# A gated scan with grouped experts: the units' instructions through the routing of the eleventh put down in front of the third early job's work

## The chip, the cores and the metric

The kernel runs on one core of one Trainium2 chip. The metric is device time in microseconds (us) from the start of the program to its end; several executions are taken and the median counts. A core has five engines with a queue of instructions each: TensorE (PE in the profile, its weight loads PEld), VectorE (DVE), ScalarE (ACT), GpSimd (POOL) and SyncE (SP), which here issues most of the DMA transfers. The engines wait for each other by semaphores.

## The reference

Two layers, one behind the other. The first is a gated scan over each of four sequences of 3648 tokens with 256 features; the second sends each of the 14592 resulting rows through one of 16 small networks.

```python
f = lower_bound + (1 - lower_bound) * sigmoid(f_logit)
for t in range(S):                                  # S = 3648, per sequence
    h = f[:, t] * h + (1 - f[:, t]) * x[:, t]
    y[:, t] = h
x = y.reshape(14592, 256)
g = argmax(x @ w_group)                             # 4 groups, weight g_w = its softmax
e = argmax(x @ w_expert[g])                         # 4 experts in a group, weight e_w
out[token] = g_w * e_w * (relu(x @ w1[g, e]) @ w2[g, e])   # 256 -> 1024 -> 256
```

## The kernel before

**Units.** The tokens are cut into 29 units of 512 (0 to 28). A unit is loaded (`p1_load`, 1 MB, tile zt; from unit 11 on by ScalarE's queue), gated on ScalarE (`p1_ta`, lines 189 and 199) and scanned on VectorE, once for each half of the features (`p1_tb`, lines 215 and 226). TensorE turns its rows (`p1_back`, two parts, line 253), computes its routing numbers (`p1_router`, line 267) and turns those (`p1_logits`, line 278). Units are routed in groups of mostly two: s1 to s6 on VectorE find each row's expert and its place in that expert's list, with one small pair of matmuls (s4, lines 313 and 314), and s7 scatters the rows, 128 at a time, into the lists xs in DRAM by indirect DMAs of GpSimd's queue (line 348). Units 9 and 10 are a group, 11 and 12 the next, and so on.

**Early jobs.** An expert's list is worked on before the scan is over. Each expert has one early job (A0 to A15) for its first rows: `EARLY` says after how many units the job's rows are taken (7, 7, 9, 9, 11, 11, 13, 15, 15, ...) and how many tiles of 128 rows they are (2, 2, 2, 2, 2, 2, 3, 3, 3, ...). At a cut u, `close_early(u)` fixes the places on VectorE and `early_rows(u)` loads the rows of all jobs of that cut (tile xr, line 805, on SP's queue); these loads wait for the scatters of all units below u. The cut 11 belongs to jobs A4 and A5, 13 to A6, 15 to A7 and A8. Behind the early jobs come the late ones, B0 to B15, for the rest of each list, once all units are routed.

**A job.** Its weights come in four pieces of 512 KB (tile st, line 823, on SP's queue, eight buffers: a piece is asked for when the piece eight places earlier has been split). Each piece is split into a high half on ScalarE (wh, line 831) and the rest on VectorE (wl, line 832). The job's rows are transposed by TensorE (line 885) and split as well (xh, line 894, on ScalarE; xl, line 895, on VectorE). The first layer goes in steps (`m1_step`; four for a job of 256 rows): twelve matmuls on lines 938 to 940, then relu on ScalarE (hh, line 943) and the low half on VectorE (hl, line 944). The second layer (`m2_step`, line 968, 24 matmuls for 128 rows) ends in a scaled copy on ScalarE (line 980) and a scatter of GpSimd's queue into the output (line 981). While a job is worked on, the next one is split and transposed.

**The order.** The units' work stands in one list of 424 items (`bgq`), in the order in which it must be put down; `marks[u]` is the number of the item `early_rows(u)`: 160 for the ninth, 212 for the eleventh, 239 for the thirteenth; `marks["order"]` is 424. In a loop over the jobs, `bg_step` puts down items between the jobs' steps so that each mark is reached by a due point, half a job before the job that needs it is prepared; `bg_to(n)` puts down all items up to n at once. `start_macro(mi + 1)` at the top of a job makes sure that the next job's rows have been asked for.

In the kernel before, the items stand like this around the third early job (A2; its steps are those of `mi == 2`): items up to 197 before A2's first step, 198 to 202 behind it, 203 to 206 behind the second, 207 to 210 behind the third, 211 to 214 behind the fourth. Item 193 and 195 are the scatters of units 9 and 10, 197 is `close_early(11)`, 212 is `early_rows(11)`.

SP's instructions keep the order in which the code puts them down for the whole kernel. TensorE's, VectorE's and ScalarE's keep it only before the loop over the jobs; in the loop the framework may let an instruction go ahead of one that was put down earlier, by when it expects their inputs. On the chip each engine then follows its own queue strictly.

Of the kernel before, what the change touches and what calls it, by code (L numbers as in the profile page):

```python
# [45 lines left out]
def gated_scan_moe(ctx: ExitStack, tc, zx, lower, wroute, wexp, out, S):  # L46
# [874 lines left out]
    def m1_step(j, ch, cs):  # L921
        if j.raw:
            return raw1(j, ch, cs)
        w = j.chunks[ch][1]
        if cs[0] == 0:
            j.hh[ch] = mo.tile([P, KF, 2 * P], F16, name="hh")
            j.hl[ch] = mo.tile([P, KF, 2 * P], BF16, name="hl")
            b, p, g = j.parts[ch][-1]
            if g > 1 and p < P // g:
                for t in (j.hh[ch], j.hl[ch]):  # L930
                    nc.vector.memset(t[:, :, w:w + P // g - p], 0.0)
        late[0] += j.kind == "B"
        pm = bank("m1" if late[0] % 2 == 0 else "p")
        xh, xl = j.xh[ch][:, :, 0:w], j.xl[ch][:, :, 0:w]
        for n, c in enumerate(cs):
            po = pm[:, n * w:(n + 1) * w]
            for k in range(KD):
                nc.tensor.matmul(po, w1_at(j.wh, k, c), xh[:, k], start=(k == 0), stop=False)  # L938
                nc.tensor.matmul(po, w1_at(j.wh, k, c), xl[:, k], start=False, stop=False)  # L939
                nc.tensor.matmul(po, w1_at(j.wl, k, c), xh[:, k], start=False, stop=(k == KD - 1))  # L940
        hi = j.hh[ch][:, cs[0]:cs[-1] + 1, 0:w]
        pv = pm[:, 0:len(cs) * w].rearrange("p (c w) -> p c w", w=w)
        nc.scalar.activation(hi, pv, AF.Relu)  # L943
        nc.vector.scalar_tensor_tensor(out=j.hl[ch][:, cs[0]:cs[-1] + 1, 0:w], in0=pv, scalar=0.0, in1=hi,  # L944
                                       op0=ALU.max, op1=ALU.subtract)
# [9 lines left out]
    def m2_step(j, ch, t, pm=None):  # L955
        b, p, g = j.parts[ch][t]
        begun = pm is not None
        pm = pm if begun else bank("m2")
        c0 = b - j.chunks[ch][0]
        q, dw = P // g, D // g  # L960
        n = p if g == 1 else q
        ts = slice(c0, c0 + n)
        if j.raw:
            raw2(j, ch, t, range(KF // 2 if begun else 0, KF), pm)
        for c in range(0 if j.raw else KF):
            for s, (h, w) in enumerate(((j.hh, j.wh), (j.hh, j.wl), (j.hl, j.wh))):
                for i in range(g):
                    nc.tensor.matmul(pm[i * q:i * q + n, 0:dw], h[ch][:, c, ts], w2_at(w, c)[:, i * dw:(i + 1) * dw],  # L968
                                     start=(c == 0 and s == 0), stop=(c == KF - 1 and s == 2),
                                     tile_position=(0, i * q) if g > 1 else None)  # L970
        o = mo.tile([P, D], F32, name="o", bufs=O_BUFS)
        if j.kind == "B":
            lt, r = j.info, b // P
            if g > 1:
                r += j.tails.index((b, p, g))
        else:
            pi = max(i for i, (a, _) in enumerate(j.pieces) if a <= b)
            lt, r = j.meta[pi], (b - j.pieces[pi][0]) // P
        s = slice(0, p if g == 1 else P)
        nc.scalar.activation(o[s, 0:dw], pm[s, 0:dw], AF.Copy, scale=lt.bitcast(F32)[s, r, 1:2])  # L980
        nc.gpsimd.indirect_dma_start(  # L981
            out=out_v[out_n[0]].rearrange("n (g d) -> (n g) d", g=g),
            out_offset=bass.IndirectOffsetOnAxis(ap=lt[s, r, 0:1], axis=0),
            in_=o[s, 0:dw], in_offset=None, bounds_check=g * N - 1, oob_is_err=False)
        out_n[0] += 1
# [19 lines left out]
    def first_parts():  # L1005
        out = []
        for (j,), u in zip(macros, PLAN):
            half = {}

            def begin(j=j, half=half):  # L1010
                half[0] = bank("m2")
                raw2(j, 0, 0, range(KF // 2), half[0])
            fs = [lambda j=j: job_xt(j, 0)]
            fs += [lambda j=j, cs=cs: m1_step(j, 0, cs) for cs in j.cols[0]]
            fs += [begin, lambda j=j, half=half: m2_step(j, 0, 0, half[0])]
            out += [(u, f) for f in fs]
        return out

    thunks, marks = p1_thunks(list(range(NU)), GROUPS, first_parts())
# [3 lines left out]
    def bg_pop():  # L1023
        done[0] += 1
        bgq.popleft()()

    def bg_to(n):
        while done[0] < n:
            bg_pop()
# [11 lines left out]
    def prep_thunks(j):  # L1041
        th = []

        def sp(i):
            if i == 2:
                live[0] += 1
            at = piece_index[(id(j), i)]
            fetch_to(max(at + 1, min(at + (4 if j.raw else STG_BUFS), pptr[0] + 2)))
            job_split(j, i)
            if i == 3 and j.kind == "B" and j.idx == 1:  # L1050
                leftovers()
            if i == 3 and j.kind == "B" and j.idx + 1 < NE:
                tail_blank(j.idx + 1)

        for i in range(4):
            f = lambda i=i: sp(i)
            f.held = i == 2
            th.append(f)
        for pi in range(len(j.pieces)):
            th.append(lambda pi=pi: job_xt(j, pi))  # L1060
        return th

    def start_macro(mi):
        mac = macros[mi]
        bg_to(marks[EARLY[mac[0].idx][0]] if mac[0].kind == "A" else marks["order"])
        for j in mac:
            if j.kind != "A" or j.idx == NE - 1:
                job_rows(j)

    def work(mac):  # L1070
        return sum(len(j.chunks) * KF + sum(len(p) for p in j.parts) for j in mac)
# [13 lines left out]
    def bg_step(q, left, n):  # L1085
        if q:
            for _ in range(-(-len(q) * n // max(1, left))):
                if q and not (getattr(q[0], "held", False) and live[0] >= 3):
                    q.popleft()()
        if bgq:  # L1090
            rate = max([(m - done[0]) / (a - now[0]) for a, m in due if a > now[0] and m > done[0]] or [0.0])
            credit[0] += rate * n
            while credit[0] >= 1 and bgq:
                credit[0] -= 1
                bg_pop()
        now[0] += n
# [13 lines left out]
    for mi, mac in enumerate(macros):  # L1110
        if mi < len(PLAN):
            continue
        q = deque()
        if mi + 1 < len(macros):
            start_macro(mi + 1)
            for j in macros[mi + 1]:
                q.extend(prep_thunks(j))
        left = work(mac)
        for j in mac:
            for ch in range(len(j.chunks)):  # L1120
                for cs in j.cols[ch]:
                    m1_step(j, ch, cs)
                    left -= len(cs)
                    bg_step(q, left - 2, len(cs))
                if pending is not None:
                    pj, pc = pending
                    for t in range(len(pj.parts[pc])):
                        m2_step(pj, pc, t)
                        left -= 1
                        bg_step(q, left - 2, 1)  # L1130
                    if pc == len(pj.chunks) - 1:
                        live[0] -= 1
                pending = (j, ch)
        while q:
            q.popleft()()
# [66 lines left out]
```

## Time and profile before

| | us |
|---|---|
| median of 3 runs (lowest to highest) | 775.78 (774.38 to 777.86) |
| the profiled execution's own time | 776.59 |
| its span (first to last instruction) | 774.8 |
| TensorE busy in it | 716.6 |
| VectorE busy in it | 533.9 |
| ScalarE busy in it | 458.8 |
| GpSimd busy in it | 286.6 |

The profile is one execution. A row of a timeline says when an instruction (or a run of equal ones) began, how long it took, its engine, line and tiles, and in brackets how long the engine had been idle before it and who ended that. A matmul's end is modelled. PEclk is the granted share of TensorE's clock: 1.00 is 2.4 GHz, 0.50 is 1.2 GHz.

### The profile page before, as it was taken

What the parts mean: (1) busy time and instruction counts of PE and PEld (TensorE: products, weight loads), DVE (VectorE), ACT (ScalarE), POOL (GpSimd) and SP (SyncE); (2) the same over time, 40 slices, a digit from 0 to 9 for tenths busy, and PEclk for the clock granted to TensorE, in tenths of its full rate; (3) what the DMA queues carried; (4) which work ended last, traced back from release to release, by engine and by line L of the source; (5) the groups of instructions that cost most, each with busy time, mean ns of one, the idle gap of its engine ahead of it and who ended that gap; (6) DMA issues with size and microseconds to landing.
All of it is one profiled execution on the core that took longest, in us unless ns stands there. A gap on an engine that the chain in (4) does not pass through costs nothing.

```text
span 774.8 us, 20906 instructions
## 1 busy us (share of the span) xinstructions
PE 716.6 (92%) x8055; PEld 633.7 (82%) x8055; DVE 533.9 (69%) x1046; ACT 458.8 (59%) x822; POOL 286.6 (37%) x272
## 2 busy tenths in 40 slices
PE   2656996989999999999999999999999999999995
PEld 1434885778888888889888898999999999999995
DVE  6898798898999976786465545555564676666640
ACT  6586785867878955455455444454555465555541
POOL 3663248276556543642111122213222322232222
PEclk9985998999999999999999999999999999999998
DMA  7998898889998845588656343553553556555300
GB/s 278 352 376 301 306 303 246 320 281 314 317 326 287 266 152 124 171 223 203 170 133 135 120 101 108 134 127 120 139 168 101 158 158 173 158 168 175 88 30 24
DMA packets 104037, 151.75 MB, mean 196 GB/s; under 512 B 63938, under 2 KB 73952, under 8 KB 100608
## 3 DMA queue, kind: packets, MB, share of 16 engines
q1 hardware_dynamic: 89248, 102.00, 45.3%
q0 software_dynamic: 11424, 30.02, 10.8%
q10 hardware_dynamic: 3264, 18.39, 6.9%
q8 instruction: 63, 1.03, 0.6%
q14 instruction: 38, 0.31, 0.1%
HBM read 112.69 MB, written 38.19 MB: 195 GB/s over the span
## 4 chain that ended last, share of the span: by engine, by line
PE 63%; DVE 11%; issue 10%; DMA 10%; POOL 4%; ACT 1%; SPq 0%; POOLq 0%; DVEq 0%; ACTq 0%
PE ps_m L968 29%; PE ps_m L938 7%; PE ps_m L939 7%; PE ps_m L940 7%; DMA xs<-rows,posi 4%; DMA zt<-in_zx_dram 3%; PE ps_p L938 3%; PE ps_p L940 3%; PE ps_p L939 3%; POOL out_dram L981 3%; DVE h L226 2%; DVE wl L832 2%; DMA xr<-xs 2%; PE ps_p L253 1%; DVE hl L944 1%
## 5 line engine op out<-in xcount | busy, mean ns | idle before, releaser
L968 PE MATMUL ps_m<-wh,hl 128*128 128x256 f16 (+4 forms) x1304 | 261.4, 251 | 0.0
L968 PE MATMUL ps_m<-wl,hh 128*128 128x256 bf16 (+4 forms) x1304 | 261.2, 250 | 0.1
L968 PE MATMUL ps_m<-wh,hh 128*128 128x256 f16 (+4 forms) x1304 | 261.1, 251 | 0.0
L968 PEld LDWEIGHTS <-hh 128*128 128x128 f16 (+2 forms) x2608 | 192.3, 99 | 23.4 <-issue 3.7
L938 PE MATMUL ps_m<-xh,wh 128*128 128x256 f16 (+11 forms) x766 | 192.7, 261 | 7.2 <-DVE hl L944 7.2
L939 PE MATMUL ps_m<-xl,wh 128*128 128x256 bf16 (+11 forms) x766 | 192.7, 261 | 0.3 <-DVE xl L895 0.3
L940 PE MATMUL ps_m<-xh,wl 128*128 128x256 f16 (+11 forms) x766 | 192.7, 261 | 0.0
L832 DVE TENSOR_TENSOR wl<-st,wh 128x1024 bf16<-128x1024 f32 x124 | 149.6, 1218 | 55.2 <-ACT wh L831 54.0
L348 POOL DMA_INDIRECT xs<-rows,posi x114 | 135.2, 1186 | 129.3 <-DVE rows L330 47.6
L981 POOL DMA_INDIRECT out_dram<-o,info x75 | 86.2, 1150 | 242.4 <-ACT o L980 221.1
L944 DVE SCALAR_TENSOR_TENSOR hl<-ps_m,hh 128x512 bf16<-128x512 f32 (+9 forms) x172 | 114.5, 668 | 74.5 <-ACT hh L943 73.7
L943 ACT ACTIVATE hh<-ps_m 128x512 f16<-128x512 f32 (+9 forms) x172 | 101.1, 588 | 65.9 <-PE ps_m L940 65.9
L831 ACT CAST wh<-st 128x1024 f16<-128x1024 f32 x124 | 128.2, 1048 | 14.7 <-PE ps_m L968 8.9
L939 PEld LDWEIGHTS <-wh 128*128 128x128 f16 x1072 | 105.4, 98 | 13.8 <-issue 6.3
L938 PEld LDWEIGHTS <-wh 128*128 128x128 f16 x1072 | 105.4, 98 | 10.2 <-issue 2.0
L940 PEld LDWEIGHTS <-wl 128*128 128x128 bf16 x1072 | 105.4, 98 | 8.0 <-issue 0.5
L968 PEld LDWEIGHTS <-hl 128*128 128x128 bf16 (+4 forms) x1304 | 103.0, 99 | 10.1 <-issue 0.2
L981 POOL DMA_INDIRECT out_dram<-o,meta x55 | 60.8, 1105 | 109.6 <-ACT o L980 98.6
L980 ACT ACTIVATE o<-ps_m,info 128x256 f32<-128x256 f32 (+4 forms) x75 | 33.1, 442 | 84.3 <-PE ps_m L968 77.0
L938 PE MATMUL ps_p<-xh,wh 128*128 128x256 f16 (+13 forms) x306 | 73.4, 252 | 0.0
L939 PE MATMUL ps_p<-xl,wh 128*128 128x256 bf16 (+13 forms) x306 | 73.3, 252 | 0.0
L940 PE MATMUL ps_p<-xh,wl 128*128 128x256 f16 (+13 forms) x306 | 73.3, 252 | 0.0
(168 smaller groups left out, 769.8 us busy)
## 6 DMA issues: line engine op xcount, KB each, us to landing
st<-in_wexp_dram SPq DMA_DIRECT2D x124, 512.0 KB, 5.0
zt<-in_zx_dram ACTq DMA_DIRECT2D x17, 1024.0 KB, 9.6
zt<-in_zx_dram SPq DMA_DIRECT2D x9, 1024.0 KB, 8.0
xs<-blank SPq DMA_DIRECT2D x26, 258.0 KB, 6.7
xr<-xs SPq DMA_DIRECT2D x11, 258.0 KB, 4.9
xr<-xs SPq DMA_DIRECT2D x16, 129.0 KB, 3.5
xr<-xs SPq DMA_DIRECT2D x32, 64.0 KB, 2.2
xs<-rows,posi POOLq DMA_INDIRECT x114, 6.0
```

What stands on the lines that cost most here:

```text
L226: nc.vector.tensor_tensor_scan(out=h[:, k, c0 - a:c1 - a], data0=ff[:, k, c0 - a:c1 - a], data1=uu[:, k, c0 - a:c1 - a], initial=init, op0 ...
L348: sc = nc.gpsimd.indirect_dma_start(out=xs_v[G["t0"] + t][:, :], out_offset=bass.IndirectOffsetOnAxis(ap=R["posi"][:, t:t + 1], axis=0), i ...
L831: nc.scalar.copy(j.wh[i], j.st[i])
L832: nc.vector.tensor_tensor(out=j.wl[i], in0=j.st[i], in1=j.wh[i], op=ALU.subtract)
L938: nc.tensor.matmul(po, w1_at(j.wh, k, c), xh[:, k], start=(k == 0), stop=False)
L939: nc.tensor.matmul(po, w1_at(j.wh, k, c), xl[:, k], start=False, stop=False)
L940: nc.tensor.matmul(po, w1_at(j.wl, k, c), xh[:, k], start=False, stop=(k == KD - 1))
L943: nc.scalar.activation(hi, pv, AF.Relu)
L944: nc.vector.scalar_tensor_tensor(out=j.hl[ch][:, cs[0]:cs[-1] + 1, 0:w], in0=pv, scalar=0.0, in1=hi, op0=ALU.max, op1=ALU.subtract)
L968: nc.tensor.matmul(pm[i * q:i * q + n, 0:dw], h[ch][:, c, ts], w2_at(w, c)[:, i * dw:(i + 1) * dw], start=(c == 0 and s == 0), stop=(c == ...
L980: nc.scalar.activation(o[s, 0:dw], pm[s, 0:dw], AF.Copy, scale=lt.bitcast(F32)[s, r, 1:2])
L981: nc.gpsimd.indirect_dma_start(out=out_v[out_n[0]].rearrange("n (g d) -> (n g) d", g=g), out_offset=bass.IndirectOffsetOnAxis(ap=lt[s, r, ...
```

## The change

At the top of the third early job (A2), before anything of it is put down, all items of the units' list up to `marks[11]` are put down at once.

```diff
@@ gated_scan_moe, the loop over the jobs @@
     for mi, mac in enumerate(macros):
         if mi < len(PLAN):
             continue
+        if mi == 2:
+            bg_to(marks[11])
         q = deque()
         if mi + 1 < len(macros):
             start_macro(mi + 1)
```

Fifteen items, 198 to 212, change their place. By engine they are: on TensorE the second part of unit 12's rows, its logits, both parts of unit 13's rows and its routing numbers; on VectorE the second scan of unit 13, the gate and first scan of unit 14, and s1 to s3 of units 11 and 12; on ScalarE unit 15's gate and the copies of what TensorE made; on ScalarE's queue the load of unit 16; on SP's queue the row loads of A4 and A5. After them `bg_step` goes on with items 213 and later by the same rule, and so puts them down earlier as well: at A4's transposes 233 items have been put down instead of 224, at A5's 247 instead of 243, and from A6 on the two orders differ by one item at most.

SP's queue, worked out from the code (W A4.3 is the fourth weight piece of A4):

```
before: ... W A4.2, blank, W A4.3, W A5.0, W A5.1, W A5.2, rows of A4 and A5, blank, W A5.3, W A6.0, W A6.1, W A6.2, W A6.3, W A7.0, rows of A6, W A7.1 ...
after:  ... W A4.2, blank, rows of A4 and A5, W A4.3, W A5.0, blank, W A5.1, W A5.2, W A5.3, W A6.0, W A6.1, W A6.2, rows of A6, W A6.3, W A7.0, W A7.1 ...
```

## Rows read from the trace of the kernel before

**Rows 1.** The page, busy time of the engines with share of the span.

```profile
PE 716.6 (92%) x8055; PEld 633.7 (82%) x8055; DVE 533.9 (69%) x1046; ACT 458.8 (59%) x822; POOL 286.6 (37%) x272
```

**Rows 2.** Windows: stretch, length, busy time by engine, granted clock, DMA share, GB/s.

```profile
104.00:200.00 96.00, 84.16 (x834) 71.97 (x833) 84.99 (x154) 71.08 (x131) 57.63 (x45) 0.95 0.89 293
200.00:700.00 500.00, 497.57 (x5770) 449.96 (x5768) 332.18 (x648) 282.88 (x494) 164.08 (x145) 1.00 0.59 169
...
127.30:134.10 6.80, 5.27 (x24) 3.68 (x25) 4.54 (x7) 1.37 (x4) 5.58 (x5) 0.50 0.83 204
...
171.70:175.10 3.40, 3.17 (x29) 2.94 (x29) 3.40 (x11) 1.17 (x2) 2.48 (x4) 0.50 0.64 210
```

**Rows 3.** Timeline of TensorE: start, duration, what, idle before it and its releaser.

```profile
128.79 1.41 PE L885 MATMUL ps_p<-ident,xr 128*128 128x128 f32 x4 [4.62 <-DMA xr<-xs]
...
140.23 0.39 PE L938 MATMUL ps_m<-xh,wh 128*128 128x256 f16 x2
...
149.03 0.27 PE L938 MATMUL ps_m<-xh,wh 128*128 128x256 f16 x1 [1.86 <-DVE hl L944]
...
171.87 0.27 PE L938 MATMUL ps_m<-xh,wh 128*128 128x128 f16 x1 [2.09 <-DVE hl L944]
...
182.54 0.36 PE L885 MATMUL ps_p<-ident,xr 128*128 128x128 f32 x1 [1.11 <-DMA xr<-xs]
```

**Rows 4.** The chain that ended last, from 105 to 140 us: start, length, what.

```profile
122.95 3.40 DMA out_dram<-o,meta
...
126.60 2.06 DMA xr<-xs
...
135.57 0.44 PE ps_p L253 x4
...
137.97 0.12 PE ps_p L278
```

**Rows 5.** Timeline of SP's queue, 98 to 135 us.

```profile
100.62 16.53 SPq L823 DMA_DIRECT2D st<-in_wexp_dram  x4
126.60 2.70 SPq L805 DMA_DIRECT2D xr<-xs  x4
```

**Rows 6.** Timeline of GpSimd, the last of the eight scatters from 105.82 on.

```profile
120.36 0.97 POOL L348 DMA_INDIRECT xs<-rows,posi  x1 [0.30 <-DMA xs<-rows,posi]
```

**Rows 7.** Timeline of VectorE, 121 to 160 us.

```profile
122.32 1.26 DVE L226 TENSOR_TENSOR_SCAN h<-zt,h 128x512 f32<-128x512 f32 x1
...
123.64 0.65 DVE L944 SCALAR_TENSOR_TENSOR hl<-ps_m,hh 128x512 bf16<-128x512 f32 x1
124.22 1.20 DVE L215 SCALAR_TENSOR_TENSOR zt<-zt 128x1024 f32<-128x1024 f32 x1
...
138.88 0.69 DVE L944 SCALAR_TENSOR_TENSOR hl<-ps_m,hh 128x512 bf16<-128x512 f32 x1 [7.04 <-ACT hh L943]
...
139.71 1.27 DVE L226 TENSOR_TENSOR_SCAN h<-zt,h 128x512 f32<-128x512 f32 x1
...
148.90 2.35 DVE L832 TENSOR_TENSOR wl<-st,wh 128x1024 bf16<-128x1024 f32 x2
...
154.03 0.69 DVE L944 SCALAR_TENSOR_TENSOR hl<-ps_m,hh 128x512 bf16<-128x512 f32 x1
...
155.30 0.31 DVE L320 TENSOR_REDUCE sm<-ex 128x40 f32<-128x160 f32 x1
```

**Rows 8.** DMA, 104 to 126.6 us: all packets; weight loads, KB each, median us to landing.

```profile
DMA packets 1797, 7.01 MB, mean 310 GB/s; under 512 B 326, under 2 KB 521, under 8 KB 1415
...
st<-in_wexp_dram SPq DMA_DIRECT2D x3, 512.0 KB, 9.1
```

**Rows 9.** DMA, 300 to 340 us: scatters, median us to landing.

```profile
xs<-rows,posi POOLq DMA_INDIRECT x14, 3.9
```

**Rows 10.** Weight loads (line 823) issued from 60 to 340 us.

```profile
DMA to landing us min/median/max: 4.7/6.3/9.1
```

**Rows 11.** The page, costliest groups: ScalarE's half of the split.

```profile
L831 ACT CAST wh<-st 128x1024 f16<-128x1024 f32 x124 | 128.2, 1048 | 14.7 <-PE ps_m L968 8.9
```

## The prediction, made before the changed kernel was run

> **What bounds the kernel now.** I read the page first: over the whole span TensorE is busy 92% of the time [rows 1], so time is won or lost where TensorE waits or is granted less than its full clock. The windows then show where that is [rows 2]. From 200 to 700 us TensorE is busy 497.57 of 500 us at full clock: whatever the order does there, the same matmuls take the same time. From 104 to 200 us, the stretch in which jobs A2 to A7 run beside the units, it is busy 84.16 of 96 us, and two pieces of that stretch have a granted clock of 0.50 (1.2 GHz instead of 2.4). The reader is to see that a change in the order around job A2 is worth what it does to these 11.8 us of waits and to the slow pieces, and that this passes straight on to the end.
>
> The timeline of TensorE names the waits [rows 3]: 4.62 us before the transposes of A4's rows at 128.79, which wait for a row load; 1.86 us and 2.09 us before first-layer steps, which wait for VectorE; 1.11 us before A7's transposes, for a row load again. The chain of waits goes through the longest of them [rows 4]: a transfer of GpSimd's queue lands at 126.35, SP can then issue the row loads of A4 and A5 at 126.60, and 2.06 us later TensorE goes on. The clock falls to 0.50 inside that wait and stays there until 134.1; 5.27 us of TensorE's work run at half speed, which costs 2.6 us [rows 2]. So this one place costs about 7.2 us.
>
> What SP was doing before that is in its own timeline [rows 5]: by 117.2 it had issued the four weight loads that stand in front (counting four per job, these are A4's last piece and A5's first three), and then it waited 9.4 us. The scatters it waits for are the eight of units 9 and 10; GpSimd issues the last one at 120.36 [rows 6], and 6.2 us later SP may go on.
>
> **What the change does to the queues.** Nothing is added or removed; items 198 to 212 of the units' list are put down in front of A2's first step instead of among A2's first three steps. Three things follow from the code.
>
> *The scatters of units 9 and 10 don't move.* They are items 193 and 195, already in front. So the last scatter still leaves GpSimd near 120.36, and SP still cannot ask for A4's rows before it lands.
>
> *SP's queue changes, and its order is kept as written.* The row loads of the eleventh stand in front of A4's last weight piece and A5's first three. These four (512 KB each) are no longer issued between 100.6 and 117.2 but after the row loads. In 104 to 126.6 the DMA moves 7.01 MB [rows 8]; three of the four belong wholly to it, 1.57 MB or 22%. The scatter's 6.2 us are measured under that load; in a quieter stretch, 300 to 340 us, scatters land after 3.9 us in the median [rows 9]. So the row loads come earlier by something between 0 and 2.3 us; I take the share of the load, 22% of 6.2, which is **1.4 us**. The Trainium skill has a rule for this ("DMA: Bandwidth & Descriptors", section "Issuing engines are not separate DMA queues"): transfers of all the issuing engines share the same 16 DMA engines and interleave. By it the 1.4 us are real and the sum below stands; if SP's loads did not slow GpSimd's scatters, this term would be 0 and the sum 1.4 us smaller. The two landing times, 6.2 and 3.9 us, agree with it.
>
> *More of the units' work stands in front of A4's transposes.* When the code comes to them, it has put down 233 items, against 224 before. For TensorE the difference is the second half of unit 14's rows, its logits and the first half of unit 15's rows: 0.44 + 0.12 + 0.44 us by rows 4, so **1.0 us** that now fills the wait instead of following it. Below nothing this can't be; it is 0 if the framework's own order already differs. That it runs units ahead of their place is visible on VectorE: the scan at 122.32, by count the second one of unit 15, stands before A3's first step at 123.64 although the code puts it down after it [rows 7].
>
> *The clock.* Of the wait 4.62 - 1.4 - 1.0 = 2.2 us stay. Rows 3 and 2 have two waits of that size. After 1.86 us the clock stayed up (the mean of 0.95 over the 96 us leaves no room for a third slow piece); at 2.09 us it fell to 0.50 and 3.17 us of work ran at half speed, a loss of 1.6 us. I take the second, 1.6 instead of 2.6, a gain of **1.0 us** (bounds 0 and 2.6).
>
> *The late weight piece.* A4's last piece is now issued behind the four row loads: 125.2 + 2.70 = 127.9. Weight loads of the early part land after 4.7, 6.3 or 9.1 us (least, median, most) [rows 10]. With the median it is there at 134.2; ScalarE's cast (1.05) [rows 11] and VectorE's difference (1.18, half of the pair at 148.90) and then, behind them in VectorE's queue, A3's third step and A4's own low half (1.27 for such a pair with its small copy, rows 7, from 154.03 to 155.30) make 137.7. TensorE began A4 at 140.23 [rows 3] and would come to it 3.4 us earlier, at 136.8. So it waits **0.9 us** again (bounds 0 with 4.7 us; 3.7 with 9.1). VectorE stood idle for 7.04 us until 138.88 in the kernel before, and this cover pays for the rest: without it every microsecond of lateness would be passed on, because the units' scans and the next steps are queued behind the piece. A5's pieces have time: they are issued within some 5 us of A4's and were split only at 148.90 [rows 7].
>
> *Later.* The sums of units 13 and 14 are put down before A4's third step and A5's rows instead of behind them, 1.27 us earlier [rows 7]; their scatters start behind them, and A7's rows wait for these scatters. The wait of 1.11 us at 182.54 goes (**1.1 us**; bounds 0 and 1.1). From job A6 on the two orders differ by one item at most, so nothing more is counted.
>
> **Sum.** 1.4 + 1.0 + 1.0 - 0.9 + 1.1 = 3.6 us less. The profiled execution took 776.59 us (its span of 774.8 and 1.8 around it): 773.0. It lies 0.81 above the median of the runs shown, 775.78; for the median that is **772.2 us**.
>
> **The rivals.**
>
> *Nothing to measure.* The scatters land when they did, the framework had run the units ahead anyway, and A4's last piece takes its median: 129.3 + 6.3 + 3.5 = 139.1, before 140.23. Then only the order of names differs: 775.8 us, within 2 either way. For it: the position of the scan at 122.32. Against it: the DMA engines really have 22% less to do in front of the scatters.
>
> *Slower: the weight piece holds two queues.* The rows are not earlier and A4's last piece, issued at 129.3 into a burst of eight weight loads, takes 9.1 us, as one did at 109.33 in the loaded stretch [rows 8]: 138.4, and VectorE is through with A4's rows at 141.9 instead of being free at 138.88. TensorE waits 1.7 us, VectorE stays 3.1 us behind, and being busy for 85 of the 89 us of rows 2's first stretch that are left without its one long gap, it passes this on to the scatters of units 13 and 14 and to A7's rows; with one more fall of the clock (1.6) that is 4.7 us: 780.5. It decides from a landing time of 7.4 us on (140.23 - 3.5 - 129.3). The Trainium skill speaks for this one ("TensorE: Matmul & The Clock Gate", the table at its head): ScalarE's and VectorE's queues are strict first in, first out. The trace agrees: the scan at 139.71 had its gate from 124.22 on and yet stood behind the step at 138.88. By that rule alone the time is the one just given.
>
> *More than forecast.* The scatters land in 3.9 us, the clock stays at 1.00 and A4's piece takes 4.7 us: 2.3 + 1.0 + 2.6 + 1.1 - 0.9 = 6.1 us, so 769.7.
>
> **How the numbers follow.** The forecast has 0.42, nothing to measure 0.22, slower 0.21, more than forecast 0.15. A change of 0.5% (3.9 us) is about what can be told from none, and the forecast lies close to that border, so its 0.42 is split in halves: faster 0.21 + 0.15 = 0.36, same 0.21 + 0.22 = 0.43, slower 0.21. The range goes from 767.5 (a little below the best case, should the 2.09 us wait shrink too) to 780.5 (the slower case); the forecast's own is 769.5 to 774.5.
>
> **What would show it.** In the profile of the changed kernel SP's row loads of A4 should stand in front of four weight loads and begin before 126; the wait before A4's transposes should be near 2 us; A4's last cast should wait for its load, and VectorE's long gap should end with that difference instead of A3's last step; the half-clock piece should be shorter; A7's transposes should not wait. The prediction is wrong if the scatters of units 9 and 10 themselves leave GpSimd at another time, if a new wait appears before A3's first steps (VectorE is nearly full there, so anything put in front of A3's splits delays them), or if the framework orders TensorE's work quite differently around A4.

## The result, and the profile of the changed kernel

The changed kernel takes 768.94 us (median of 6 runs, 765.25 to 769.77), the kernel before, on the same chip, 776.29 (6 runs): a ratio of 0.990 (95% interval 0.987 to 0.992), 7.4 us less. The profiled execution took 769.22 against 776.59, again 7.4 less. The time lies inside the range that was given, 3.3 us below the forecast, and most of the way to it was not the predicted one.

The first rows are the page's busy times and the windows (stretch, length, busy time by engine, granted clock, DMA share, GB/s), which answer to [rows 1, 2].

```profile
PE 712.9 (93%) x8055; PEld 632.1 (82%) x8055; DVE 534.0 (70%) x1046; ACT 457.8 (60%) x822; POOL 287.6 (37%) x272
...
104.00:200.00 96.00, 88.57 (x920) 77.30 (x910) 92.90 (x175) 75.73 (x142) 61.45 (x48) 0.96 0.90 320
200.00:700.00 500.00, 497.98 (x5763) 450.43 (x5762) 327.66 (x633) 280.17 (x489) 162.99 (x145) 1.00 0.58 166
123.80:130.70 6.90, 4.51 (x21) 3.31 (x21) 6.80 (x14) 3.13 (x5) 4.11 (x5) 0.51 0.64 165
...
171.70:175.10 3.40, 3.40 (x34) 3.05 (x33) 3.40 (x6) 3.40 (x7) 1.92 (x2) 1.00 0.99 393
```

From 200 us on nothing has changed: the same work starts about 7.4 us earlier and keeps this distance to the end. All of the gain is made between 104 and 200 us. There TensorE is busy for 4.4 us more (88.57 instead of 84.16) and VectorE for 7.9 us more (92.90 instead of 84.99). VectorE has 3.1 us left of 96, TensorE 7.4: VectorE is the fuller engine of the stretch now. One of the two pieces at half clock is gone (from 171.7 to 175.1 the clock is now 1.00), the other has moved from 127.3 to 123.8.

TensorE's timeline (start, duration, what, idle before it and its releaser) answers to [rows 3]:

```profile
121.39 0.27 PE L938 MATMUL ps_m<-xh,wh 128*128 128x256 f16 x1 [2.54 <-ACT xh L894]
125.90 0.37 PE L938 MATMUL ps_m<-xh,wh 128*128 128x256 f16 x1 [4.24 <-DVE hl L944]
...
127.63 0.37 PE L939 MATMUL ps_m<-xl,wh 128*128 128x256 bf16 x1 [0.29 <-DVE xl L895]
...
133.25 0.64 PE L885 MATMUL ps_p<-ident,xr 128*128 128x128 f32 x4
...
176.05 0.40 PE L885 MATMUL ps_p<-ident,xr 128*128 128x128 f32 x2
```

The 4.62 us before A4's transposes are gone (133.25 has no wait), and so are the 1.86, the 2.09 and the 1.11. In their place stands a wait that the kernel before did not have: 2.54 + 4.24 = 6.8 us at A3's first step. This is by 2.2 us the longer wait of the two, and still the kernel is faster. The timeline of SP answers to [rows 5], and that of VectorE to [rows 7]:

```profile
123.71 2.69 SPq L805 DMA_DIRECT2D xr<-xs  x4
126.51 2.25 SPq L823 DMA_DIRECT2D st<-in_wexp_dram  x4
```

```profile
113.65 0.19 DVE L336 TENSOR_TENSOR both<-ps_p,both 128x32 f32<-128x32 f32 x1 [1.06 <-PE ps_p L314]
...
115.96 0.68 DVE L944 SCALAR_TENSOR_TENSOR hl<-ps_m,hh 128x512 bf16<-128x512 f32 x1
116.56 1.27 DVE L226 TENSOR_TENSOR_SCAN h<-zt,h 128x512 f32<-128x512 f32 x1
117.75 2.33 DVE L832 TENSOR_TENSOR wl<-st,wh 128x1024 bf16<-128x1024 f32 x2
...
126.89 0.69 DVE L895 TENSOR_TENSOR xl<-ps_p,xh 128x512 bf16<-128x512 f32 x1
...
137.79 2.35 DVE L832 TENSOR_TENSOR wl<-st,wh 128x1024 bf16<-128x1024 f32 x2
```

The rows of A4 and A5 are asked for at 123.71 instead of 126.60, in front of four weight loads, as forecast (the blank that the plan of SP's queue put behind the second of them stands behind the fourth). On VectorE the first two splits of A3's weights begin at 117.75; in the kernel before that pair began at 108.10:

```profile
108.10 2.33 DVE L832 TENSOR_TENSOR wl<-st,wh 128x1024 bf16<-128x1024 f32 x2
```

The fifteen items stand in front of them now, and A3's low half (xl) comes only at 126.89. That is the new wait of TensorE. What the reader is to see is what is no longer there: VectorE's idle time of 7.04 us until 138.88 [rows 7]. In the changed kernel VectorE never waits for more than 1.1 us between 104 and 200 us.

### The profile page after: what moved, and what is told of

Same layout as the page of the kernel before. It is cut to its first block, busy times and chain, and to the rows that moved or that the text cites. A ratio compares the mean times of both kernels' runs of the same rounds, so it can differ in the third digit from the quotient of the medians.

```text
span 767.5 us, 20904 instructions
## 1 busy us (share of the span) xinstructions
PE 712.9 (93%) x8055; PEld 632.1 (82%) x8055; DVE 534.0 (70%) x1046; ACT 457.8 (60%) x822; POOL 287.6 (37%) x272
## 4 chain that ended last, share of the span: by engine, by line
PE 69%; DVE 11%; DMA 8%; issue 7%; POOL 2%; ACT 2%; SPq 1%; POOLq 0%; DVEq 0%; ACTq 0%
PE ps_m L968 31%; PE ps_m L938 7%; PE ps_m L939 7%; PE ps_m L940 7%; DMA zt<-in_zx_dram 4%; PE ps_p L938 3%; PE ps_p L940 3%; PE ps_p L939 3%; DVE wl L832 3%; DVE h L226 3%; PE ps_p L253 2%; POOL out_dram L981 2%; PE ps_m L916 1%; PE ps_p L267 1%; DMA xs<-rows,posi 1%
## 5 line engine op out<-in xcount | busy, mean ns | idle before, releaser
L348 POOL DMA_INDIRECT xs<-rows,posi x114 | 130.7, 1147 | 122.8 <-DVE rows L330 41.4
L981 POOL DMA_INDIRECT out_dram<-o,meta x55 | 66.1, 1202 | 107.6 <-ACT o L980 95.5
```

Source lines behind the costliest of these rows:

```text
L348: sc = nc.gpsimd.indirect_dma_start(out=xs_v[G["t0"] + t][:, :], out_offset=bass.IndirectOffsetOnAxis(ap=R["posi"][:, t:t + 1], axis=0), i ...
L981: nc.gpsimd.indirect_dma_start(out=out_v[out_n[0]].rearrange("n (g d) -> (n g) d", g=g), out_offset=bass.IndirectOffsetOnAxis(ap=lt[s, r, ...
```

## The experiments

Two theories were set against each other. **ROWS**, the larger part of the prediction's sum: the gain comes from A4's rows being asked for earlier, from the wait behind it and its slow clock. **VECTOR** (an expectation may say LEAD, for the lead that the units' work gets): the gain comes from the units' work that VectorE does where it stood idle for 7 us. e5 to e8 ran on one chip (before: 776.35 us, 12 runs). e1 to e4 and e9 to e12 ran on two chips on which every kernel took about 5% longer (before: 814.11, 25 runs, and 815.83, 29 runs); their ratios are to those runs, and the change itself was not run there, which limits what they say.

**The change again (e5).**

> The changed kernel itself, beside its halves and the version with the splits first, so that all of them stand against the same runs. The chip of the first four experiments was slower throughout (the kernel before took 814 us on it), so their ratios need the change's own ratio beside them. Expected on an ordinary chip: 0.987 to 0.992 as first measured, with a long wait before A3's first step and none before A4's transposes.

768.62 us, 0.990 (0.988 to 0.992). TensorE waits 3.42 + 3.35 us at the same place, and VectorE's longest wait between 104 and 200 us is 1.06 us.

**The row loads alone (e6, and e1 on a slower chip).**

```diff
+        if mi == 2:
+            early_rows(11)
```

and item 212 does nothing when it comes.

> The row loads of A4 and A5 alone ahead in SP's queue, once more. Theory ROWS: ratio near 0.991. Theory LEAD (what counts is that the units' list is ahead from A2 to A5, so that VectorE never runs empty and no sum or scatter is late): ratio 0.997 to 1.002, the wait before A4's transposes shrinks, and its time comes back as waits for VectorE behind it.

774.79 us, 0.998 (0.997 to 0.999): 1.6 us of the 7.4. Windows, TensorE's timeline and VectorE's:

```profile
104.00:200.00 96.00, 85.25 (x848) 72.74 (x846) 85.56 (x158) 71.71 (x131) 59.51 (x45) 0.95 0.86 295
```

```profile
123.79 0.36 PE L885 MATMUL ps_p<-ident,xr 128*128 128x128 f32 x1 [1.39 <-DMA xr<-xs]
124.88 0.62 PE L885 MATMUL ps_p<-ident,xr 128*128 128x128 f32 x3 [0.74 <-DMA xr<-xs]
...
128.56 0.37 PE L938 MATMUL ps_m<-xh,wh 128*128 128x256 f16 x1 [2.51 <-DVE hl L944]
```

```profile
127.81 0.69 DVE L944 SCALAR_TENSOR_TENSOR hl<-ps_m,hh 128x512 bf16<-128x512 f32 x1 [5.87 <-ACT hh L943]
```

TensorE's wait for A4's rows falls from 4.62 to 1.39 + 0.74. But VectorE's gap only shrinks from 7.04 to 5.87, TensorE then waits 2.51 us for VectorE, and little of what was won comes through. In the profiled execution, which is 2.1 us shorter than that of before, the first copy of an output tile (line 980) already starts 1.6 us earlier, at 102.02 instead of 103.59, ahead of the place in question. So ROWS explains 1.6 us at most. On the slower chip (e1) the same kernel gave 1.001 (0.997 to 1.005).

> SP's queue as in the change (the row loads of A4 and A5 in front of the four weight loads), all other items of the units at their old places. Theory ROWS (the gain is that A4's rows come earlier, because the scatters land without the weight loads beside them): TensorE's wait of 4.62 us in front of A4's transposes shrinks to 2 us or less and most of the 7.4 us are there, ratio near 0.991. Theory VECTOR (the gain is that VectorE, the fuller engine of this stretch, no longer stands idle for 7 us behind A3's last step, because the units' work stands in front): the gap of VectorE stays above 4 us and no more than 2 us are gained, ratio 0.997 to 1.001.

**The units' work alone (e7, and e2 on a slower chip).** The change, but the row loads are asked for where they were, behind A5's third weight piece.

```diff
+        if mi == 2:
+            bg_to(marks[11])             # item 212 does nothing
...
+                    if mi == 2 and cs[0] == 6:
+                        early_rows(11)
```

> The units' items 198 to 211 ahead, the row loads at their old place behind A5's third weight load. Theory LEAD alone: ratio 0.987 to 0.993. If both halves are needed (the row loads then stand behind weight loads that wait for A3's splits, which the units' work delays on VectorE): ratio 0.995 or more, with the row loads several us later than in the changed kernel.

767.94 us, 0.989 (0.987 to 0.991): the whole gain without the moved row loads.

```profile
104.00:200.00 96.00, 88.66 (x910) 77.43 (x910) 92.73 (x175) 75.33 (x141) 60.57 (x48) 0.95 0.94 318
```

```profile
120.88 0.37 PE L938 MATMUL ps_m<-xh,wh 128*128 128x256 f16 x1 [2.41 <-ACT xh L894]
125.52 0.37 PE L938 MATMUL ps_m<-xh,wh 128*128 128x256 f16 x1 [4.27 <-DVE hl L944]
```

```profile
123.64 2.80 SPq L805 DMA_DIRECT2D xr<-xs  x4
```

The windows and the wait are those of the change, and even SP asks for the rows at the same time (123.64): the scatters decide that, and no longer the place in SP's queue. With e6 this settles, for this chip, which half of the change gains: it is the units' work. It doesn't settle by which engine, because the items lie on TensorE, ScalarE and VectorE alike.

On the slower chip e2 is the same kernel, and there it gained nothing, against its expectation by VECTOR: 1.001 (0.999 to 1.004). The number is the one that ROWS gave, but not for its reason: TensorE doesn't wait for A4's rows there.

> The other half: the units' items 198 to 211 in front of A2's first step, the row loads of A4 and A5 at their old place behind A5's third weight load in SP's queue. Theory VECTOR: nearly all of the gain stays, since TensorE comes to A4's transposes only near 133 us and rows that land at 129 are early enough; ratio 0.988 to 0.993. Theory ROWS: the gain is gone, ratio 0.997 or more, and TensorE waits for A4's rows.

**A3's splits first (e8, and e4 on a slower chip).** The change's new wait comes from A3's splits standing behind the units' work. So the row loads and A3's four splits are put down first, then the items (against the kernel before; item 212 again does nothing).

```diff
+        if mi == 2:                      # behind start_macro(3)
+            early_rows(11)
+            for _ in range(4):
+                q.popleft()()
+            bg_to(marks[11])
```

> The row loads, then A3's four splits, then the items up to 212. If the wait before A3's first step is only an order on VectorE: faster than the changed kernel by 3 to 7 us, ratio 0.980 to 0.986. If VectorE is simply full: as the changed kernel, 0.987 to 0.992.

767.07 us, 0.988 (0.986 to 0.989). Windows and TensorE's timeline:

```profile
104.00:200.00 96.00, 90.93 (x926) 77.71 (x918) 93.08 (x176) 76.15 (x143) 64.57 (x48) 0.98 0.89 320
120.00:130.70 10.70, 8.93 (x101) 7.63 (x91) 10.70 (x18) 6.39 (x13) 7.82 (x7) 1.00 0.70 207
139.00:141.00 2.00, 2.00 (x12) 1.37 (x10) 2.00 (x7) 0.25 (x2) 1.70 (x2) 0.50 1.18 377
```

```profile
117.37 0.65 PE L253 MATMUL ps_p<-ident,h 128*128 128x128 f32 x4 [0.84 <-DVE both L336]
...
123.81 0.27 PE L938 MATMUL ps_m<-xh,wh 128*128 128x256 f16 x1 [1.57 <-DVE hl L944]
...
137.84 0.27 PE L938 MATMUL ps_m<-xh,wh 128*128 128x256 f16 x1 [1.21 <-DVE hl L944]
```

TensorE's wait of 6.8 us is down to 0.84 + 1.57, and the half clock is gone from that place. But part of both has moved on: TensorE now waits 1.21 us at 137.84, for VectorE, and from 139 to 141 its clock is 0.50. The kernel is 1.5 us faster than the change, with intervals that overlap, which is the second side of the expectation (VectorE is full, and the wait moves to another step). VectorE is as busy as in the change (93.08 against 92.90), and TensorE puts through about as many matmuls (926 against 920). On the slower chip this kernel gave 0.988 (0.982 to 0.994), the only one of the eight runs on the two slower chips that was clearly faster.

> The row loads first, then the four splits of A3's weights, then the items up to 212, all in front of A2's first step. In the changed kernel TensorE waits 2.54 and 4.24 us before A3's first step, for hl of A2 and A3's splits, which stand behind the units' work on VectorE. If that wait is the price of the change and only an order on VectorE, it shrinks to 2 us or less and the kernel is 3 to 7 us faster than the changed one, ratio to the kernel before 0.980 to 0.986. If VectorE is simply full there, the wait moves to another step and the time stays within 2 us of the changed kernel, ratio 0.987 to 0.992.

**VectorE's work done twice (e9 in the changed kernel, e10 in the kernel before; a slower chip).** The four low halves of A4's weights are computed twice, with the same values: some 4.8 us more for VectorE. The output is the same.

```diff
-        nc.vector.tensor_tensor(out=j.wl[i], in0=j.st[i], in1=j.wh[i], op=ALU.subtract)
+        for _ in range(2 if j.kind == "A" and j.idx == 4 else 1):
+            nc.vector.tensor_tensor(out=j.wl[i], in0=j.st[i], in1=j.wh[i], op=ALU.subtract)
```

> The kernel before with the same four instructions done twice. There they stand right in front of VectorE's idle time of 7.04 us (until 138.88). Theory VECTOR: 4.8 us of the 7.04 are filled with what is not needed, nothing behind is late, so 0 against the kernel before (within 1 us). Rival: VectorE's instructions cost time wherever they stand, because A4's splits lie on the path of A4: 2 to 4.8 us slower than the kernel before, as much as in the changed kernel.

> The changed kernel with VectorE's half of A4's four weight splits done twice (the same values written twice): 4 x 1.2 us more on VectorE, 4.8 us, while A3 is worked on; nothing else is added. Theory VECTOR (the stretch from 104 to 200 us is bound by VectorE, which in the changed kernel is idle for only 2.7 of 100 us): all of it but at most 2.7 us is passed on, so 2.1 to 4.8 us slower than the change, 771 to 773.4. Rival TENSOR (TensorE's waits and clock decide, VectorE has room beside it): no more than 1 us slower, 768 to 769.6.

In the kernel before (e10): 811.81 against 815.83, 0.996 (0.992 to 1.000). The added 4.8 us cost nothing, so the rival (2 to 4.8 us slower) has fallen, and VectorE's timeline shows where they went:

```profile
128.60 4.61 DVE L833 TENSOR_TENSOR wl<-st,wh 128x1024 bf16<-128x1024 f32 x4
133.15 0.67 DVE L945 SCALAR_TENSOR_TENSOR hl<-ps_m,hh 128x512 bf16<-128x512 f32 x1
133.75 4.61 DVE L833 TENSOR_TENSOR wl<-st,wh 128x1024 bf16<-128x1024 f32 x4
...
141.88 0.69 DVE L945 SCALAR_TENSOR_TENSOR hl<-ps_m,hh 128x512 bf16<-128x512 f32 x1 [2.25 <-ACT hh L944]
```

The gap in front of A3's last step is 2.25 us, where it was 7.04 in the kernel before on the ordinary chip: 4.8 less, just what was added. (The kernel before left no trace on this chip. These lines are one below its own.) So the gap was free room on VectorE, which is the half of VECTOR that this run tests.

In the changed kernel (e9): 815.63, 1.001 (0.998 to 1.005). Set against e10 it is 0.5% slower, with an uncertainty as large as that, and the changed kernel without the doubling was not run on that chip. Its expectation is neither met nor refuted. VectorE's timeline shows that it wasn't full there: it waited for 8.19 us before the sums of units 11 and 12 ("remote": the profile has no record of what ended the wait).

```profile
126.45 0.19 DVE L336 TENSOR_TENSOR both<-ps_p,both 128x32 f32<-128x32 f32 x1 [8.19 <-remote]
```

**The lead given back (e11, and e3 on the other slower chip).** The whole change, then no item until the old plan has caught up, at A2's end.

```diff
-        if bgq:
+        if bgq and not (now[0] < 24 and done[0] >= marks[11]):
```

> The whole change, and then no further item of the units is put down until the old plan has come to item 212, at A2's end. The lead is taken once and given back before A3 begins. Theory VECTOR: VectorE has units' work ahead of A3's first steps, but from A3 on the order is the old one, so the 7-us gap behind A3's last hh is there again; between the two kernels and nearer to the kernel before, ratio 0.995 to 1.0. Rival ONCE (it is the fifteen items in A2 that matter, not the lead kept afterwards): as the change, 0.988 to 0.992.

> The whole change, but after it no further item is put down until A2's fourth step, where the kernel before had come to the same item; from there both lists run alike. It asks whether the gain comes from the fifteen items themselves or from the lead that the list keeps afterwards (items 213 to 250 up to ten places earlier). Theory VECTOR as I hold it (the gap of VectorE is filled once, by the fifteen items): the gain stays within 2 us, ratio 0.988 to 0.993. If the lead is what counts (sums of units 11 to 14 and so the scatters earlier, no waits behind A4): ratio 0.995 or more, and waits of 1 to 2 us near 149, 172 and 182 us are back.

1.002 (0.998 to 1.006) and 1.001 (0.998 to 1.005): no gain. The two expectations have VECTOR on opposite sides: for e3, which came first, it said that the fifteen items once are enough and the gain stays, and that missed; for e11 it said that the lead must be kept. No gain agrees with the second wording, but e2, with the lead kept, had no gain on such a chip either. Whether the lead kept matters or the fifteen items once stays open.

**Twice the lead (e12).** Splits first, and at the top of A3 everything up to the thirteenth's row loads as well.

```diff
+        if mi == 3:
+            bg_to(marks[13])
```

> A3's splits first as in the run before, then all items up to 212, and at the top of A3 all items up to the thirteenth's row loads (239) as well: the lead is doubled. Theory VECTOR: VectorE had 2.65 us left between 100 and 200 us, so at most 1 us more than splits first alone, ratio 0.986 to 0.9875; slower where A4's splits come too late behind the units' work, up to 0.99. Rival LEAD (every item put ahead gains, as the fifteen did): 4 us or more beyond splits first, ratio below 0.983.

823.77 us, 1.012 (1.007 to 1.017): 1.2% slower than before, where splits first alone was 1.2% faster on a chip like it. "Every item put ahead gains" has fallen. The size missed VECTOR's bound of 0.99 too. VectorE isn't full in it: it waits 7.54 us, before the sums of the routing that was put ahead this time, so this run doesn't test what a doubled lead does to a full VectorE:

```profile
146.35 0.19 DVE L336 TENSOR_TENSOR both<-ps_p,both 128x32 f32<-128x32 f32 x1 [7.54 <-remote]
```

## Why the prediction came out

**The sum.** 3.6 us were forecast, 7.4 came. The direction and the range held; the terms, one by one:

*Earlier row loads (forecast 1.4).* SP asked 2.9 us earlier, twice the forecast, but not by the forecast's way. From the start of the eighth scatter (117.19) to SP's row loads (123.71) it is 6.5 us, against 6.2 before: not shorter, although no weight load is issued there any more. The scatters themselves went out earlier, the eighth 3.2 us earlier. The prediction named this as something that would make it wrong. Its own way does show in e6, where the row loads alone are ahead: there it is 3.0 us, a fall of 3.3 where at most 2.3 were allowed for. The lines of the change, then those of e6:

```profile
115.30 0.33 ACTq L179 DMA_DIRECT2D zt<-in_zx_dram  x1
117.19 1.42 POOL L348 DMA_INDIRECT xs<-rows,posi  x1 [0.30 <-issue]
```

```profile
118.59 0.98 POOL L348 DMA_INDIRECT xs<-rows,posi  x1 [0.30 <-issue]
121.56 2.69 SPq L805 DMA_DIRECT2D xr<-xs  x4
125.85 0.34 ACTq L179 DMA_DIRECT2D zt<-in_zx_dram  x1
```

What differs is the load of a unit (1 MB), which the change moves as well and for which the prediction had no term: in the change it is issued 1.9 us before the eighth scatter, in e6 behind the row loads. In the eight traces with such a load 1 to 3.1 us before the eighth scatter the time is 4.2 to 6.8 us, in the five without one 2.9 to 3.6 (in e2 SP was held up by weight loads). No run moved that load alone. Measured by itself in e6, asking earlier is worth 1.6 us at most; in e7 its place in the queue is worth nothing.

*More units' work in front (forecast 1.0).* **This is the term that was mis-sized.** It counted only TensorE's share: 1.0 us of transposes and logits that fill its wait. VectorE's share was seen ("stood idle for 7.04 us until 138.88") and used only as cover for a late weight piece. It was the largest thing in the stretch. The gap arose because A3's last relu on ScalarE came late, while the units' scans and gates were queued on VectorE behind that step's low half. TensorE's wait for A4's rows is one part of this: A3's last matmuls ended only at 133.8. The other part is ScalarE's own order. In the kernel before the relu stands behind two copies of the units' work, which wait for TensorE's transposes of line 253 and line 278, and these come late in TensorE's queue:

```profile
136.05 0.59 ACT L255 COPY rows<-ps_p 128x512 f32<-128x512 f32 x1 [5.22 <-PE ps_p L253]
138.12 0.23 ACT L279 COPY Lg<-ps_p 128x80 f32<-128x80 f32 x1 [1.49 <-PE ps_p L278]
...
138.24 0.60 ACT L943 ACTIVATE hh<-ps_m 128x512 f16<-128x512 f32 x1
```

So the relu ran 4.4 us after its matmuls had ended. With the units' work in front, VectorE's busy time from 104 to 200 us rises by 7.9 us, about the 7.4 us of the result. By itself this names no engine, since a kernel that is 7 us ahead at 200 us has done more of everything by then; but e7 (this term alone) gives the whole gain, and e10 shows that the gap was free room. By TensorE's own account one comes to 6.4: 4.4 us less waiting, 1.6 from the half-clock piece that is gone (3.17 us at half speed [rows 2]), and 0.4 from the one that moved (4.51 us of work in it instead of 5.27). These are the same microseconds seen from the engine that waits.

*The clock (forecast 1.0).* The slow piece at A4 did not go; it moved to the new wait, and 0.4 us are saved. The other one, which the prediction left alone, went: 1.6 us.

*The late weight piece (forecast a cost of 0.9).* Not seen. A4's last cast ran without a wait for its load, as one of a pair that VectorE took at 137.79 without idling. The slower rival, which hung on this piece, did not come (its 3.1 us for VectorE are 3.0 by its own figures, 141.9 less 138.88).

*A7's wait (forecast 1.1).* Gone, as said (176.05 has no wait), and with it the two waits of 1.86 and 2.09 us for VectorE, which had no term.

*The new wait.* The last sentence of the prediction names it: "a new wait appears before A3's first steps (VectorE is nearly full there, so anything put in front of A3's splits delays them)". It came, with 6.8 us, and was priced at nothing. It costs little, and VectorE works through it, for 7.00 of the 7.10 us from 118.8 to 125.9, in which TensorE is busy for 0.32:

```profile
118.80:125.90 7.10, 0.32 (x6) 0.19 (x2) 7.00 (x14) 4.51 (x11) 2.54 (x2) 0.86 0.41 144
```

Taking most of it away at this place (e8) brings 1.5 us.

**What stays open.** That VectorE's room is what the units' work filled is argued from e7, e8 and e10; no run moved the items of one engine alone. Laid side by side, the fourteen traces fit it on all the chips: the five that belong to a gain of 1% or more (the change twice, e7, e8, and e4 on a slower chip) are those in which VectorE never waits for more than 1.3 us between 104 and 200 us. In the other nine its longest wait is 2.25 us (e10, where the added work fills the gap) to 8.25. This is a comparison made afterwards and not a test.

On a slower chip units' work alone brought nothing (e2). The traces of the slower chips show instructions as long as elsewhere, but pauses of TensorE for which no releaser is found ("issue" in these rows of its waits from 100 to 700 us in e9: what, total, times, longest),

```profile
PE ps_m L969 <- issue: 11.3, 18, 1.5
PE ps_m L939 <- DVE hl L945: 9.9, 5, 4.9
```

where the changed kernel on the ordinary chip has none of the first kind. And in e2, e3, e9 and e11 VectorE waits 7.2 to 8.3 us before the sums of units 11 and 12 (line 336), which takes 1.06 us in the changed kernel above. Such a wait takes back the whole gap. It isn't TensorE coming late to the routing's small matmuls: in e2 they began at 117.14, and VectorE went on only 7.4 us later, where it takes 0.2 us in the changed kernel.

```profile
117.14 0.19 PE L314 MATMUL ps_p<-scn,ones 128*128 128x16 bf16 x1
```

```profile
124.56 0.19 DVE L336 TENSOR_TENSOR both<-ps_p,both 128x32 f32<-128x32 f32 x1 [8.25 <-remote]
```

What ends the wait is in no trace. e4, on the chip of e2, has no such wait and is the one that gained there.

## What to carry to other kernels

When a stretch is bounded by waits of the busiest engine, look at the other engines' idle time in the same stretch, not only at the waits: here the second engine had 11 us of slack in 96, seven of them in one gap, and work of its own queued just behind that gap. On the ordinary chip filling it was worth about its length, and a longer wait on TensorE at another place cost little. Look also at what stands in front of the late step on the engine between, ScalarE here: the relu waited behind copies that could have come earlier. And measure it on the chip that counts: on a slower one the same half of the change gained nothing, and a doubled lead (e12) lost 1.2%.

## What the runs showed that was not expected

The time from the eighth scatter to the row loads that wait for it did not shrink in the change, where the weight loads stand behind them (6.5 us, against 6.2 with the weight loads in front), and fell to 3.0 in e6, where the unit's load stands behind them too.

A wait of 6.8 us on TensorE with half the clock behind it (0.51 from 123.8 to 130.7) and one of 2.4 us with none at that place (1.00 from 120 to 130.7, e8; 0.50 from 139 to 141) differ by 1.5 us at the end (with overlapping intervals); VectorE was nearly full in both.

The same kernel differs by 5% from chip to chip (776 against 814 and 816 us), and a change that gives 1.1% on one of them (e7) gave nothing on another (e2).
